# Loading x in fp32 by the hardware queue, with cast and reordering on GpSimd

## The chip, the core and the metric

The kernel runs on one core of one Trainium2 chip. The core has five engines with a queue of instructions each: TensorE (PE in the profile; its weight loads are PEld), VectorE (DVE), ScalarE (ACT), GpSimd (POOL) and SyncE (SP), which here only issues transfers. Sixteen DMA engines move data between the chip's main memory (DRAM) and the on-chip memory (SBUF, 96 or 128 partitions of a tile at a time). Matrix products land in a third memory, PSUM, from which ACT and DVE evict them. The metric is device time in microseconds (us) for one execution; less is better.

## What is computed

```python
x: 8 x 3072 x 256, fp32
X = np.fft.fft(x, axis=1)
X = np.fft.fft(X, axis=2)
h0 = X.real.astype(np.float32).reshape(24576, 256)
h = np.maximum(np.maximum(h0 @ w1, h0 @ w2), h0 @ w3)     # w1, w2, w3: 256 x 768
out = (h @ w_out).astype(np.float32)                      # w_out: 768 x 256
```

A two-dimensional Fourier transform of each of 8 batches, of which the real part is kept, is followed by a layer that takes the maximum of three products, and by an output product.

## The kernel before

**Tiling of the transform.** The 3072 rows of a batch are split as 24 x 128 (`a`, `bb`) and the 256 features as 4 x 64 (`g`, `dl`). The tile x0 holds one batch in bf16: partition g*24 + a (96 of them), and in each partition 128 rows of 64 features. A transform over `a` is a product with a 96 x 96 block matrix, `m24blk`. The function `fnet` does it with 64 matmuls (L270), one for each of the 64 features: the 128 values of that feature in x0 are the weights, which TensorE loads first (PEld L270), and `m24blk` is what streams through them, 96 columns. Before the change the weights of one matmul lie 64 elements, 128 bytes, apart. Five matmuls (in the last but one group, four) fill one PSUM tile, and ACT copies it to the tile ub (L272); there are 13 such groups in a batch and two PSUM buffers. DVE then adds and subtracts mirrored features ("folds", L280 to L297) to give zE and zO, TensorE multiplies these by cosine and sine tables (L318 to L334, again with strided weights, steps of 24 and 26 elements), and ACT evicts tE and tO (L329). POOL makes reversed copies of both, tEr and tOr (L339, L340).

**The layers.** In the main loop each batch has three blocks of 512 positions. `unit_plus`, `unit_minus` and `unit_out` compute the three-way maximum for a block and its mirror: 512-column matmuls L349, L350 and L357, an ACT eviction with Relu into stmp (L363) and a DVE maximum (L364) of a PSUM tile and stmp into hp and hm. `l2_block` makes the output product of a finished block (L367, L369, L372: 256 columns each); DVE copies the result to ot (L392, four buffers) and SP stores it (L399). These second-layer matmuls wait in a list, `l2_queue`, and are issued between the matmuls of the next block and the next batch's transform.

**Preparation.** Before the first batch DVE and ACT make the tables (`m24blk`, cos_t, sin_t, nsin_t, md) from index tiles that POOL writes (kidx, dvec). `prep_first` and `prep_second` fold the feature transform into the weights: DVE differences v_bf (L228), matmuls L232, ACT evictions, and a DVE scaling gD (L237).

**Loading x.** `load_x0` issues 16 transfers for a batch from POOL's queue (L105): four chunks of 32 rows, each for four feature groups, 96 KB each in DRAM. The runs that lie together in DRAM are 64 features of fp32, 256 bytes, and the transfer itself turns them into bf16. There are two x0 tiles, so batch b+2 is loaded when the transform of batch b has read its tile. At the start POOL's order is written out by hand (`tc.manual_schedule`): the first x chunk, the two index tiles, the other x chunks, six weight transfers (L139), w_out (L142), and batch 1's x. Elsewhere a scheduler at build time fixes the order of every engine's queue from dependencies and program order; at run time each queue is executed in that order.

Of the kernel before, what the change touches and what calls it, by code (L numbers as in the profile page):

```python
# [9 lines left out]
FP32 = mybir.dt.float32  # L10
BF16 = mybir.dt.bfloat16
# [2 lines left out]
ALU = mybir.AluOpType  # L14

ROUND = 12582912.0


def _cond_sub(nc, pool, v, thresh, tag):
# [15 lines left out]
def kernel(  # L35
# [16 lines left out]
    nc = tc.nc  # L52

    B, S, D = x.shape
# [11 lines left out]
    ps_f = ctx.enter_context(tc.tile_pool(name="ps_f", bufs=2, space=bass.MemoryType.PSUM))  # L66
    ps_l1 = ctx.enter_context(tc.tile_pool(name="ps_l1", bufs=2, space=bass.MemoryType.PSUM))
    ps_o = ctx.enter_context(tc.tile_pool(name="ps_o", bufs=2, space=bass.MemoryType.PSUM))
    x0_pool = ctx.enter_context(tc.tile_pool(name="x0", bufs=2))
    u_pool = ctx.enter_context(tc.tile_pool(name="ubuf", bufs=1))  # L70
    z_pool = ctx.enter_context(tc.tile_pool(name="zbuf", bufs=1))
    t_pool = ctx.enter_context(tc.tile_pool(name="tbuf", bufs=2))
    h_pool = ctx.enter_context(tc.tile_pool(name="hbuf", bufs=2))
    out_pool = ctx.enter_context(tc.tile_pool(name="outbuf", bufs=4))

    m24blk = consts.tile([96, 96], BF16, tag="m24blk")
    md = [consts.tile([128, 256], BF16, name=f"md{fc}", tag=f"md{fc}") for fc in range(2)]
# [16 lines left out]
    dif = consts.tile([128, 1], FP32, tag="dif")  # L94
    t_mid = consts.tile([128, 2, B], BF16, tag="t_mid")

    def load_x0(b, between):
        x0 = x0_pool.tile([96, 128 * 64], BF16, name="x0", tag="x0")
        xr = x[b].rearrange("(a bb) (g dl) -> g a bb dl", bb=128, g=4)
        x0v = x0.rearrange("p (bb dl) -> p bb dl", dl=64)  # L100
        for ch in range(4):
            if ch in between:
                between[ch]()
            for g in range(4):
                nc.gpsimd.dma_start(  # L105
                    out=x0v[g * 24:(g + 1) * 24, ch * 32:(ch + 1) * 32, :],
                    in_=xr[g, :, ch * 32:(ch + 1) * 32, :])
        return x0

    gen_pool_cm = tc.tile_pool(name="gen", bufs=1)  # L110
    gen = gen_pool_cm.__enter__()
# [11 lines left out]
    kidx = gen.tile([128, 13 * 128], FP32, tag="kidx")  # L123
    dvec = gen.tile([128, 128], FP32, tag="dvec")

    def between():

        nc.gpsimd.iota(kidx, [[1, 13], [24, 128]], base=0, channel_multiplier=0,
                       allow_small_or_imprecise_dtypes=True)
        nc.gpsimd.iota(dvec, [[1, 64], [64, 2]], base=0, channel_multiplier=0,  # L130
                       allow_small_or_imprecise_dtypes=True)

    with tc.manual_schedule(engines={mybir.EngineType.Pool}):
        x0_tiles = {0: load_x0(0, {1: between})}


        for jh in range(2):
            for wsrc, wdst in ((moe_w1, w1_bf), (moe_w2, w2_bf), (moe_w3, w3_bf)):
                nc.gpsimd.dma_start(  # L139
                    out=wdst.rearrange("p (fc j) -> p fc j", fc=2)[:, :, jh * 384:(jh + 1) * 384],  # L140
                    in_=wsrc.rearrange("(fc p) j -> p fc j", fc=2)[:, :, jh * 384:(jh + 1) * 384])
        nc.gpsimd.dma_start(out=wout_bf.rearrange("p (jc c) -> p jc c", jc=NJC),  # L142
                            in_=moe_w_out.rearrange("(jc p) c -> p jc c", jc=NJC))
        x0_tiles[1] = load_x0(1, {})


    amod = gen.tile([96, 1], FP32, tag="amod")
    nc.vector.tensor_copy(amod, pidx[0:96])
# [24 lines left out]
    for (dst, shift) in ((cos_t, 768.0), (sin_t, 0.0)):  # L173
        v = gen.tile([128, 13 * 128], FP32, name="v", tag="v", bufs=2)
        q = gen.tile([128, 13 * 128], FP32, name="q", tag="q", bufs=2)
        nc.vector.tensor_scalar(out=v, in0=kidx, scalar1=pidx, scalar2=shift,
                                op0=ALU.mult, op1=ALU.add)
        nc.vector.tensor_scalar(out=q, in0=v, scalar1=1.0 / 3072.0, scalar2=ROUND,
                                op0=ALU.mult, op1=ALU.add)
        nc.vector.tensor_scalar(out=q, in0=q, scalar1=ROUND, scalar2=-3072.0,  # L180
                                op0=ALU.subtract, op1=ALU.mult)
        nc.vector.tensor_tensor(out=v, in0=v, in1=q, op=ALU.add)
        nc.scalar.activation(out=dst, in_=v, func=AX.Sin,
                             scale=float(2.0 * math.pi / 3072.0))
    nc.vector.tensor_scalar(out=nsin_t, in0=sin_t, scalar1=-1.0, scalar2=None,
                            op0=ALU.mult)

# [22 lines left out]
                            op0=ALU.mult, op1=ALU.add)  # L210
    nc.vector.tensor_scalar(out=dif, in0=sgn, scalar1=1.0, scalar2=None, op0=ALU.subtract)
    gen_pool_cm.__exit__(None, None, None)

    zO_tiles = [consts.tile([128, 128 * 26], BF16, name=f"zO{i}", tag=f"zO{i}")
                for i in range(1)]
# [4 lines left out]
    def prep_first():  # L220

        for jh in range(2):
            cs = slice(jh * 384, (jh + 1) * 384)
            for i, (wv, vv) in enumerate(((w2_bf, v2_bf), (w3_bf, v3_bf))):
                w3d, v3d, w13d = (t.rearrange("p (fc j) -> p fc j", fc=2)[:, :, cs]
                                  for t in (wv, vv, w1_bf))
                tc.keep_in_program_order(
                    nc.vector.tensor_tensor(out=v3d, in0=w3d, in1=w13d, op=ALU.subtract))  # L228
                for (half, dst) in ((0, gE[i]), (1, gO[i])):
                    psg = ps_f.tile([128, 512], FP32, name="psg", tag="ps")  # L230
                    for fc in range(2):
                        nc.tensor.matmul(  # L232
                            psg[:, 0:384], md[fc][:, half * 128:(half + 1) * 128],
                            vv[:, fc * DFF + jh * 384: fc * DFF + jh * 384 + 384],
                            start=(fc == 0), stop=(fc == 1))
                    nc.scalar.copy(out=dst[:, cs], in_=psg[:, 0:384])
                nc.vector.tensor_scalar(out=gD[i][:, cs], in0=gO[i][:, cs], scalar1=dif,  # L237
                                        scalar2=None, op0=ALU.mult)
# [23 lines left out]
                                op0=ALU.mult)  # L262

    def fnet(b, x0):
        x0r = x0.rearrange("p (bb dl) -> p bb dl", dl=64)
        ub = u_pool.tile([128, 64 * 96], BF16, name="ub", tag="ub")
        for (d0, d1) in DLS:
            ps1 = ps_f.tile([128, 512], FP32, name="ps1", tag="ps")
            for i in range(d1 - d0):
                nc.tensor.matmul(ps1[:, i * 96:(i + 1) * 96], x0r[:, :, d0 + i], m24blk,  # L270
                                 start=True, stop=True)
            nc.scalar.copy(out=ub[:, d0 * 96:d1 * 96], in_=ps1[:, 0:(d1 - d0) * 96])  # L272

# [79 lines left out]
    def unit_minus(pses, to, jc):  # L353

        js = slice(jc * 128, (jc + 1) * 128)
        for i, pse in enumerate(pses):
            nc.tensor.matmul(pse, gD[i][:, js], to, start=False, stop=True,  # L357
                             skip_group_check=True)

    def unit_out(pses, dst, n):  # L360
        stmp = h_pool.tile([128, TOKB], BF16, name="stmp", tag="stmp")
        src3 = pses[1][:, 0:n]
        nc.scalar.activation(out=stmp[:, 0:n], in_=pses[0][:, 0:n], func=AX.Relu)  # L363
        nc.vector.tensor_tensor(out=dst, in0=src3, in1=stmp[:, 0:n], op=ALU.max)  # L364
# [53 lines left out]
    def l2_some(n):  # L418
        while n > 0 and l2_queue:
            try:  # L420
                next(l2_queue[0])
                n -= 1
            except StopIteration:
                l2_queue.pop(0)

    for b in range(B):
        tt = fnet(b, x0_tiles.pop(b))
        if b == 0:
            prep_first()
        tE, tO = tt[0]  # L430
        prev = None

        def finish(prev):
            pses, to, jc, hm = prev
            unit_minus(pses, to, jc)
            unit_out(pses, hm[:, jc, ::-1], TOKB)

        for blk in range(3):
            cs = slice(blk * TOKB, (blk + 1) * TOKB)
            hp = h_pool.tile([128, NJC, TOKB], BF16, name="hp", tag="hp")  # L440
            hm = h_pool.tile([128, NJC, TOKB], BF16, name="hm", tag="hm")
            for jc in range(NJC):
                pses = unit_plus(tE[:, cs], tO[:, cs], jc, TOKB)
                unit_out(pses, hp[:, jc, :], TOKB)
                if prev is not None:
                    finish(prev)
                prev = (pses, tO[:, cs], jc, hm)
                l2_some(11)
            l2_some(1000)
            if blk == 2:  # L450
                finish(prev)
            if b == 0 and blk == 0:
                prep_second()
            l2_queue.append(l2_block(b, blk, hp, hm, tt))
            if blk == 0 and b + 2 < B:
                x0_tiles[b + 2] = load_x0(b + 2, {})
            if blk == 1 and b == B - 1:
                l2_queue.append(l2_mid())

# [30 lines left out]
```

## Time and profile before

| What | Value |
|---|---|
| median of 3 runs | 500.57 us (499.67 to 501.51) |
| span of the profiled execution, first to last instruction | 497.1 us |
| mean granted TensorE clock | 0.993 |
| x transfers on POOL, L105 | 128, 109.5 us busy |
| first matmul of the transform, L270 | starts at 27.46 us |
| x0 matmuls, L270 | 512, 57.4 us busy |
| POOL copies tEr, L339 | 8, 1471 ns each |
| folds, L280, zE and zO | 160, 260 to 473 ns each |
| store issues on SP, L399 | 208, median 431 ns |

A row of the profile has a source line, the engine, the operation, the tile it writes and the tile it reads, their shapes, and how often it occurs; then the busy time in us, the mean duration of one in ns, and the engine's idle time just before with what ended it. Matmuls are pipelined, so one's duration is longer than its distance to the next; the distance of their starts is what TensorE pays. The page also shows the span in 40 slices of 12.4 us, with a digit for the busy tenths of each. A timeline row begins with the start and the duration in us, and ends, in brackets, with idle time and its releaser. 3.5 us of the runs' median lie outside the profiled span.

### The profile page before, as it was taken

The page shows a single profiled execution, that of the slowest core. Times are in us where ns is not written, and L with a number is a line of the kernel's source. Part 1 is how long each engine was busy: PE and PEld are TensorE (multiplying, and loading weights), DVE is VectorE, ACT ScalarE, POOL GpSimd, SP SyncE. Part 2 cuts the span into 40 slices and gives each one's busy share as a digit, 9 for nine tenths or more (in the row PEclk, how much of TensorE's full clock was granted, in tenths as well). Part 3 has the DMA queues.
Part 4 walks back from the last instruction along what each step waited for, and adds up shares of the span by engine and source line. Part 5 has one row for each costly group of instructions (what it writes and reads, how often), then busy time and mean ns, then how long its engine had stood idle before and what let it go on. Part 6 is the DMA issues. An engine that isn't in the chain of part 4 may idle for free.

```text
span 497.1 us, 9195 instructions
## 1 busy us (share of the span) xinstructions
PE 453.5 (91%) x3408; PEld 315.6 (63%) x3408; DVE 320.4 (64%) x662; ACT 260.9 (52%) x472; POOL 140.6 (28%) x160
## 2 busy tenths in 40 slices
PE   0056999999999999999999999999999999999995
PEld 0055447785568657785669666875669566866664
DVE  8834674657676576657666567657675666667663
ACT  1355652575436653575446644665457644765440
POOL 9979800029000750029000840048000100020000
PEclk9999899999999999999999999999999999999998
DMA  8999992219921692219911793119911022102122
GB/s 48 75 164 99 98 32 86 84 44 108 105 86 66 59 133 99 73 44 109 126 65 65 74 123 102 65 46 120 134 64 65 22 65 84 65 22 65 65 84 86
DMA packets 163436, 40.05 MB, mean 81 GB/s; under 512 B 136512, under 2 KB 163392, under 8 KB 163392
## 3 DMA queue, kind: packets, MB, share of 16 engines
q0 software_dynamic: 135536, 14.30, 70.6%
q1 hardware_dynamic: 27856, 25.18, 16.1%
q8 instruction: 26, 0.43, 0.4%
q14 instruction: 18, 0.15, 0.1%
HBM read 28.31 MB, written 25.17 MB: 108 GB/s over the span
## 4 chain that ended last, share of the span: by engine, by line
PE 78%; DVE 3%; ACT 2%; POOL 2%; DMA 1%; issue 1%; DVEq 0%; ACTq 0%
PE po L372 23%; PE pse L349 12%; PE pse L357 11%; PE pse L350 11%; PE ps L270 8%; PE po L367 4%; PE po L369 4%; POOL x L105 2%; PE ps L318 2%; DMA x<-in_x_dram 1%; PE ps L324 1%; PE ps L326 1%; ACT stmp L363 1%; PE ps L321 1%; DVE zE L280 1%
## 5 line engine op out<-in xcount | busy, mean ns | idle before, releaser
L363 ACT ACTIVATE stmp<-pse 128x512 bf16<-128x512 f32 (+1 forms) x294 | 167.7, 588 | 164.3 <-PE pse L350 128.6
L364 DVE TENSOR_TENSOR hp<-pse,stmp 128x512 bf16<-128x512 f32 x144 | 99.1, 690 | 99.1 <-PE pse L357 39.8
L105 POOL DMA_DIRECT2D x<-in_x_dram x128 | 109.5, 863 | 8.1 <-DMA x<-in_x_dram 3.6
L349 PE MATMUL pse<-tE,gE 128*128 128x512 bf16 x288 | 108.8, 379 | 1.7 <-DVE hm L364 0.7
L350 PE MATMUL pse<-tO,gO 128*128 128x512 bf16 x288 | 109.1, 380 | 0.0
L364 DVE TENSOR_TENSOR hm<-pse,stmp 128x512 bf16<-128x512 f32 x144 | 99.0, 687 | 11.8 <-ACT stmp L363 9.3
L357 PE MATMUL pse<-tO,gD 128*128 128x512 bf16 x288 | 94.8, 380 | 1.1 <-ACT stmp L363 0.6
L339 POOL COPY tEr<-tE 128x1536 bf16<-128x1536 bf16 x8 | 11.8, 1471 | 289.1 <-ACT tE L329 289.1
L372 PE MATMUL po<-wout_bf,hp 128*128 128x256 bf16 x576 | 92.6, 272 | 0.0
L372 PE MATMUL po<-wout_bf,hm 128*128 128x256 bf16 x576 | 89.1, 272 | 0.1
L270 PE MATMUL ps<-m24blk,x 96*128 96x96 bf16 x512 | 57.4, 250 | 28.8 <-DMA w_bf<-in_moe_w_dram 27.5
L270 PEld LDWEIGHTS <-x 96*128 96x128 bf16 x512 | 55.9, 199 | 33.1 <-DMA w_bf<-in_moe_w_dram 27.4
L392 DVE COPY ot<-po 128x512 f32<-128x512 f32 x96 | 65.5, 684 | 14.5 <-PE po L372 13.8
L372 PEld LDWEIGHTS <-hm 128*128 128x128 bf16 x576 | 56.1, 99 | 17.3 <-DVE hm L364 0.4
L372 PEld LDWEIGHTS <-hp 128*128 128x128 bf16 x576 | 56.2, 100 | 14.2
L272 ACT CAST ub<-ps 128x480 bf16<-128x480 f32 (+1 forms) x104 | 55.4, 554 | 15.6 <-PE ps L270 13.3
L357 PEld LDWEIGHTS <-gD 128*128 128x128 bf16 x288 | 28.1, 98 | 29.8 <-issue 1.5
L350 PEld LDWEIGHTS <-gO 128*128 128x128 bf16 x300 | 29.4, 98 | 27.1 <-issue 12.2
L349 PEld LDWEIGHTS <-gE 128*128 128x128 bf16 x300 | 29.5, 99 | 21.1 <-issue 2.6
L280 DVE TENSOR_TENSOR zE<-ub 128x240 bf16<-128x240 bf16 (+2 forms) x80 | 20.2, 311 | 33.9 <-ACT ub L272 33.9
L367 PE MATMUL po<-gw,tE 128*128 128x256 bf16 x96 | 26.2, 272 | 0.0
L369 PE MATMUL po<-gwr,tOr 128*128 128x256 bf16 x96 | 26.2, 272 | 0.0
(99 smaller groups left out, 359.5 us busy)
## 6 DMA issues: line engine op xcount, KB each, us to landing
out_dram<-ot SPq DMA_DIRECT2D x176, 128.0 KB, 1.7
x<-in_x_dram POOLq DMA_DIRECT2D x128, 96.0 KB, 6.7
out_dram<-ot SPq DMA_DIRECT2D x24, 64.0 KB, 6.7
w_bf<-in_moe_w_dram POOLq DMA_DIRECT2D x6, 192.0 KB, 6.2
out_dram<-ot SPq DMA_DIRECT2D x8, 63.0 KB
wout_bf<-in_moe_w_out_dram POOLq DMA_DIRECT2D x1, 384.0 KB, 8.6
out_dram<-ot SPq DMA_DIRECT2D x1, 8.0 KB
```

Source lines behind the costliest of these rows:

```text
L105: nc.gpsimd.dma_start(out=x0v[g * 24:(g + 1) * 24, ch * 32:(ch + 1) * 32, :], in_=xr[g, :, ch * 32:(ch + 1) * 32, :])
L270: nc.tensor.matmul(ps1[:, i * 96:(i + 1) * 96], x0r[:, :, d0 + i], m24blk, start=True, stop=True)
L272: nc.scalar.copy(out=ub[:, d0 * 96:d1 * 96], in_=ps1[:, 0:(d1 - d0) * 96])
L349: nc.tensor.matmul(pse[:, 0:n], gE[i][:, js], te, start=True, stop=False)
L350: nc.tensor.matmul(pse[:, 0:n], gO[i][:, js], to, start=False, stop=True)
L357: nc.tensor.matmul(pse, gD[i][:, js], to, start=False, stop=True, skip_group_check=True)
L363: nc.scalar.activation(out=stmp[:, 0:n], in_=pses[0][:, 0:n], func=AX.Relu)
L364: nc.vector.tensor_tensor(out=dst, in0=src3, in1=stmp[:, 0:n], op=ALU.max)
L367: nc.tensor.matmul(po, te, gw[:, 0:256], start=True, stop=False)
L369: nc.tensor.matmul(po, to, wo, start=False, stop=False)
L372: nc.tensor.matmul(po, hcols(jc), wout_bf[:, jc * 256:(jc + 1) * 256], start=False, stop=(jc == NJC - 1))
L392: nc.vector.tensor_copy(out=ot, in_=po)
```

## The change

x is loaded in fp32 by SP's queue into a new tile xs, one for each chunk (four buffers, 96 x 2048). `cast_x` copies a chunk into x0 as bf16 and writes it with features outermost and the 128 rows adjacent, so that the 128 weights of one L270 matmul lie side by side. POOL does the casts, except for 44 of the 64 features of chunk 3 of batch 0, which DVE does. At the start the index tiles come first on POOL; the weight transfers stay on POOL and follow the casts. Batch 1's load waits for the last weight transfer. In the loop, batch b+1 is cast and batch b+2 loaded after block 0 of batch b. The pools of hp, hm, stmp and ot are opened after the preparation's temporary tiles have been given back.

```diff
+AFTER = mybir.DependencyInfo(mybir.DependencyClass.Sync, mybir.DependencyReason.DATA)
...
+    xs_pool = ctx.enter_context(tc.tile_pool(name="xs", bufs=4))
...
-    h_pool = ctx.enter_context(tc.tile_pool(name="hbuf", bufs=2))
-    out_pool = ctx.enter_context(tc.tile_pool(name="outbuf", bufs=4))
...
-    def load_x0(b, between):
-        x0 = x0_pool.tile([96, 128 * 64], BF16, name="x0", tag="x0")
+    def load_x(b, after=None):
+        chunks = []
         xr = x[b].rearrange("(a bb) (g dl) -> g a bb dl", bb=128, g=4)
-        x0v = x0.rearrange("p (bb dl) -> p bb dl", dl=64)
         for ch in range(4):
-            if ch in between:
-                between[ch]()
+            xs = xs_pool.tile([96, 32 * 64], FP32, name="xs", tag="xs")
+            xsv = xs.rearrange("p (bb dl) -> p bb dl", dl=64)
             for g in range(4):
-                nc.gpsimd.dma_start(
-                    out=x0v[g * 24:(g + 1) * 24, ch * 32:(ch + 1) * 32, :],
+                ld = nc.sync.dma_start(
+                    out=xsv[g * 24:(g + 1) * 24],
                     in_=xr[g, :, ch * 32:(ch + 1) * 32, :])
-        return x0
+                if after is not None:
+                    tc.add_manual_dep(ld.ins, after.ins.name, AFTER, reason="weights first")
+            chunks.append(xs)
+        return chunks
+
+    def cast_x(x0, ch, xs, engine, d0=0, d1=64):
+
+        dst = x0.rearrange("p (dl bb) -> p dl bb", bb=128)[:, d0:d1, ch * 32:(ch + 1) * 32]
+        src = xs.rearrange("p (bb dl) -> p dl bb", dl=64)[:, d0:d1, :]
+        if engine is nc.scalar:
+            engine.copy(out=dst, in_=src)
+        else:
+            engine.tensor_copy(dst, src)
+
+    def new_x0():
+        return x0_pool.tile([96, 64 * 128], BF16, name="x0", tag="x0")
...
+    raw = {0: load_x(0)}
+    x0_tiles = {0: new_x0()}
+
+    with tc.manual_schedule(engines={mybir.EngineType.Pool}):
         nc.gpsimd.iota(kidx, [[1, 13], [24, 128]], base=0, channel_multiplier=0,
                        allow_small_or_imprecise_dtypes=True)
         nc.gpsimd.iota(dvec, [[1, 64], [64, 2]], base=0, channel_multiplier=0,
                        allow_small_or_imprecise_dtypes=True)
-
-    with tc.manual_schedule(engines={mybir.EngineType.Pool}):
-        x0_tiles = {0: load_x0(0, {1: between})}
+        for ch in range(3):
+            cast_x(x0_tiles[0], ch, raw[0][ch], nc.gpsimd)
         for jh in range(2):
             for wsrc, wdst in ((moe_w1, w1_bf), (moe_w2, w2_bf), (moe_w3, w3_bf)):
-                nc.gpsimd.dma_start(
+                wld = nc.gpsimd.dma_start(
...
+            if jh == 0:
+                cast_x(x0_tiles[0], 3, raw[0][3], nc.gpsimd, 44, 64)
         nc.gpsimd.dma_start(out=wout_bf.rearrange("p (jc c) -> p jc c", jc=NJC),
                             in_=moe_w_out.rearrange("(jc p) c -> p jc c", jc=NJC))
-        x0_tiles[1] = load_x0(1, {})
...
+    cast_x(x0_tiles[0], 3, raw.pop(0)[3], nc.vector, 0, 44)
+    raw[1] = load_x(1, after=wld)
+
     nc.vector.tensor_scalar(out=nsin_t, in0=sin_t, scalar1=-1.0, scalar2=None,
                             op0=ALU.mult)
...
     gen_pool_cm.__exit__(None, None, None)
+    h_pool = ctx.enter_context(tc.tile_pool(name="hbuf", bufs=2))
+    out_pool = ctx.enter_context(tc.tile_pool(name="outbuf", bufs=4))
...
     def fnet(b, x0):
-        x0r = x0.rearrange("p (bb dl) -> p bb dl", dl=64)
+        x0r = x0.rearrange("p (dl bb) -> p dl bb", bb=128)
...
-                nc.tensor.matmul(ps1[:, i * 96:(i + 1) * 96], x0r[:, :, d0 + i], m24blk,
+                nc.tensor.matmul(ps1[:, i * 96:(i + 1) * 96], x0r[:, d0 + i, :], m24blk,
                                  start=True, stop=True)
...
-            if blk == 0 and b + 2 < B:
-                x0_tiles[b + 2] = load_x0(b + 2, {})
+            if blk == 0 and b + 1 < B:
+                x0_tiles[b + 1] = new_x0()
+                for ch, xs in enumerate(raw.pop(b + 1)):
+                    cast_x(x0_tiles[b + 1], ch, xs, nc.gpsimd)
+                if b + 2 < B:
+                    raw[b + 2] = load_x(b + 2)
```

More of the change, by code (lines that the diff above doesn't have):

```diff
@@ L124 @@
     dvec = gen.tile([128, 128], FP32, tag="dvec")
-    def between():
+    raw = {0: load_x(0)}
+    x0_tiles = {0: new_x0()}
+    with tc.manual_schedule(engines={mybir.EngineType.Pool}):
         nc.gpsimd.iota(kidx, [[1, 13], [24, 128]], base=0, channel_multiplier=0,
```

## The prediction

> **What bounds the kernel now.** I read four views, from the whole to the single instruction. First the page: busy time by engine and the span in 40 slices.
>
> ```profile
> PE 453.5 (91%) x3408; PEld 315.6 (63%) x3408; DVE 320.4 (64%) x662; ACT 260.9 (52%) x472; POOL 140.6 (28%) x160
> ...
> PE   0056999999999999999999999999999999999995
> ...
> POOL 9979800029000750029000840048000100020000
> ```
>
> The reader should see two regimes. TensorE (PE) does nothing for two slices (12.4 us each), half work for two, and is then full to the end. So a microsecond is saved either before about 53 us, or by making TensorE's own work shorter; POOL is idle two thirds of the time and bounds nothing after the start. The chain of waits says the same: 78% of it is PE.
>
> Second, the timeline of the first 48 us, POOL, PE and DVE:
>
> ```profile
> 7.24 15.68 POOL L105 DMA_DIRECT2D x<-in_x_dram  x12
> ...
> 22.91 4.27 POOL L139 DMA_DIRECT2D w_bf<-in_moe_w_dram  x6
> 27.23 0.83 POOL L142 DMA_DIRECT2D wout_bf<-in_moe_w_out_dram  x1
> 27.43 1.04 PEld L270 LDWEIGHTS <-x 96*128 96x128 bf16 x11 [27.43 <-DMA w_bf<-in_moe_w_dram]
> ...
> 44.73 3.21 DVE L237 TENSOR_SCALAR gD<-gO,dif 128x384 bf16<-128x384 bf16 x1 [6.00 <-ACT gO L236]
> 44.94 1.48 POOL L339 COPY tEr<-tE 128x1536 bf16<-128x1536 bf16 x1
> 46.35 1.47 POOL L340 COPY tOr<-tO 128x1536 bf16<-128x1536 bf16 x1
> ```
>
> PE starts at 27.4 us. The page names a weight DMA as releaser, but L270 does not read weights: it needs the last of sixteen x transfers, whose issue on POOL ends at 22.9 us and which lands some 4.5 us later (median for x: 6.7 us). Issue by POOL sets the start. The gD row matters later: the other three gD took 0.31 to 0.47 us, this one 3.21, and it ended when POOL's two copies did.
>
> Third, the steady state, where the first Fourier step (L270) of batch 3 runs between second-layer matmuls (L372):
>
> ```profile
> 210.00 0.57 PE L270 MATMUL ps<-m24blk,x 96*128 96x96 bf16 x5
> 210.41 0.27 PE L369 MATMUL po<-gwr,tOr 128*128 128x256 bf16 x1
> 210.52 0.38 PE L372 MATMUL po<-wout_bf,hm 128*128 128x256 bf16 x2
> 210.74 0.57 PE L270 MATMUL ps<-m24blk,x 96*128 96x96 bf16 x5
> 211.14 0.28 PE L372 MATMUL po<-wout_bf,hm 128*128 128x256 bf16 x1
> 211.26 0.57 PE L270 MATMUL ps<-m24blk,x 96*128 96x96 bf16 x5
> ...
> 210.08 1.08 ACT L272 CAST ub<-ps 128x480 bf16<-128x480 f32 x2 [0.17 <-PE ps L270]
> ```
>
> Two groups of five take 210.00 to 211.26 = 1.26 us and hold four matmuls of 256 columns at 0.109 us (0.436). The ten small ones take the other 0.82, so 0.082 each, twice what their columns need (96/256 x 0.109 = 0.041). ACT evicts the pair in 1.08 and waits 0.17 for PE. PE is the bound here, and in it the weight load. Fourth, the page's groups of weight loads:
>
> ```profile
> L270 PEld LDWEIGHTS <-x 96*128 96x128 bf16 x512 | 55.9, 199 | 33.1 <-DMA w_bf<-in_moe_w_dram 27.4
> ...
> L372 PEld LDWEIGHTS <-hm 128*128 128x128 bf16 x576 | 56.1, 99 | 17.3 <-DVE hm L364 0.4
> ```
>
> The x weights are read with a step of 64 elements (128 bytes) and take 199 ns; hm's, adjacent, take 99.
>
> **The change, part by part.**
>
> Removed: 128 x issues of 0.81 to 0.86 us on POOL (109.5 us). In the steady state they are off the path. The spacing of the tEr copies gives the batch period: 54.7 and 54.8 us in the last two batches with loads, 54.4 in the one without. I take 0.35 us for five periods, **-1.8 us** (bounds 0, and -4.9 from the mean of all five loaded periods, 55.4).
>
> Row and feature order swapped: L270 now reads 128 adjacent weights. No row shows this at 96 partitions. Weights with a 52-byte step (zO) follow one another every 0.066 us even when 64 columns or one are multiplied; adjacent weights should be no slower. With 0.066 a pair takes 0.66 + 0.436 = 1.10 us, just above ACT's 1.08. That is -0.16 per pair, 6.5 pairs a batch: -1.04, and for seven batches **-7.3 us** (bounds: 0 if the step is not the cause; with ACT as the bound 0.18 x 6.5 x 7 = -8.2). In batch 0 a pair takes 1.25 us with PE and ACT waiting for each other; I take 0.1 x 6.5, **-0.7** (0 to -1.0).
>
> Added on SP: 128 issues. The nearest row, a store issue, is 0.43 us; sixteen are 6.9 us and not the limit. How fast small rows land is: a batch is 96 x 128 = 12,288 runs of 256 bytes. Lower bound: POOL issued 13 transfers of a batch at 0.81 us without waiting, 16 x 0.81 = 12.9 us. Upper: 70.6% x 16 x 497.1 us / 135,536 packets = 41.4 ns a packet, on 16 engines 31.8 us. In between, the last three issues of a batch (122.18, 123.36, 124.48) came 1.15 us apart, two of them after waiting for an x DMA: 18.4 us a batch, which I take, being the same runs. From 1.0 us, with 1.7 us to land (a store's), chunks arrive at 7.3, 11.9, 16.5 and 21.1 us.
>
> Added on POOL: casts of 96 x 2048. The tEr copy gives 1470 ns / 1536 elements, so 1.96 us at least; the source has a step of 256 bytes, and the only stepped-to-adjacent ratio in the trace is the weight load's, 209 ns (median for x) to 99, 2.1, so 4.1 us at most. The step is what sets this copy apart, so I take 4.1. [...]
>
> Start: iotas end by 3.9 us (no x issue ahead of them). Casts run 7.3-11.4, 11.9-16.0, 16.5-20.6; three weight issues of 0.71 to 22.7; POOL's 20/64 of chunk 3, 1.3 us, to 24.0. VectorE (DVE) casts 44/64 of it, 1408 elements: at the row of the 128x256 conversions (0.29 us) 1.6 us, doubled for the step 3.3, so 21.1 to 24.4. Ahead of it stands DVE's table chain, 9.4 us (9.23 to 18.65 now), which can begin near 6 us. If it slips between casts it costs nothing; if every cast locks it out it ends at 6 + 9.4 + 12.3 = 27.7 and PE starts at 31. I take 24.4 plus one table operation of 1.1: 25.5, **-1.9 us** (bounds: load 12.9 us gives 18.9, -8.5; load 31.8 gives 37.8, +10.4). The rest of the weights leave POOL by 27 us and land by 33; L228 reads them at 38 now, so they stay hidden with 3 us to spare. The load of batch 1, behind them on SP, takes to about 52; its use is at 96.
>
> Next in line is preparation: v_bf and gD, eight DVE operations between 38 and 56 us that PE waits for. Batch 1's casts can fall there. I put in half a cast, **+2.0** (0 to 8.2, two casts).
>
> Steady: four casts, 16.4 us, are free if they follow tOr (111.4 to 127.8 in batch 1), as the x issues do now: between 106 and 155 us DVE reads PSUM as one input and makes no folds. SP now waits for each cast before it loads the next chunk, with stores behind it; three output copies (105.9, 114.8, 120.7) fall in that time, and there are four buffers. Zero for both.
>
> Sum: -1.8 - 7.3 - 0.7 - 1.9 + 2.0 = -9.7; span 497.1 to 487.4. The median of the runs is 3.5 us over the profiled span: **490.9 us**. Own range of this case 484 to 497.
>
> **Rivals.**
>
> *The load is quick* (18.9 us to PE): 490.9 - 6.6 = 484. For: the issues of 0.81 us on POOL are gone, and a store on SP issues in 0.43. Against: the waits on x DMA at the end of each issue burst.
>
> *The weight step is not the cause*: 490.9 + 8.0 = 499. For: 199 ns is latency, and loads overlap. Against: the 0.082 us pitch.
>
> *Casts hold the folds* (the slower side). DVE's folds (L280) end PE's wait for L318, and the cover is spent: PE idles 0.41 us there already (104.6 to 105.04). If the casts of a later batch stand ahead of tEr on POOL, they meet the folds at 104, and gD shows DVE held through two POOL copies in a row. One cast a batch: 4.1 x 6 = +24.6, 516 us; all four: +98. It decides from 2.0 us a batch on. Against: the x issues now stand behind tOr although their buffer is free at 103. [...]
>
> *The load is slow* (31.8 us): PE starts at 37.8, 490.9 + 12.3 = 503.
>
> *SP holds the stores*: one cast beyond the four buffers, again 4.1 x 6, 515.
>
> That a later x arrives too late for its cast is excluded by 55 us of lead.
>
> **How the numbers follow.** Forecast 0.48, quick load 0.12, step not the cause 0.10, folds held 0.15, slow load 0.11, stores held 0.04. Predicted is the forecast's 491. Leaving out the two cases near 515 leaves 0.81: 481 to 508, with the spread of the others. A difference under 0.5% (2.5 us) can't be told from none: faster 0.62 (forecast, quick load, a little of the third), same 0.13, slower 0.25.
>
> **What would show it.** PE's first L270 at 25.5 us; L270 pairs of 1.10 us and PEld of x near 99 ns; POOL casts of 4.1 us, after tOr; folds still 0.26 to 0.47 us; period near 53. It is wrong if a fold row has a maximum of microseconds, if PE waits for ot, or if the x loads on SP land more than 2 us apart.

## The result and the profile after

| | median of the runs | ratio to the kernel before (95%) | span of the profiled run, clock |
|---|---|---|---|
| before | 500.87 us (4 runs) | | 497.1 us, 0.993 |
| after | 526.86 us (519.5 to 530.6, 4 runs) | 1.0424 [1.0362, 1.0485] | 528.8 us, 0.940 |

The changed kernel is slower by 4.2%, where 491 us was predicted. The ratio goes by the two runs at 519.5 and 523.4 us (mean 521.4, clock 0.955 and 0.949); the profile is of a slower run, at 530.6 us, so the 31.7 us that its span is longer than the 497.1 before show where time goes, and what each cause is worth is taken from the experiments.

The page of the changed kernel, engines and 40 slices (13.2 us each):

```profile
span 528.8 us, 9309 instructions
...
PE 453.2 (86%) x3408; PEld 310.1 (59%) x3408; DVE 339.3 (64%) x663; ACT 260.6 (49%) x472; POOL 150.6 (28%) x64
...
PE   0045499979998899979997999989997999999995
...
PEclk9999679969999799979998899979997999999999
```

PE's busy time is the same as before (453.5), but not its place. The row of nines now has a hole early (the 4 in slice 5) and a dip that comes back every 4.4 slices, which is a batch period; below each, the granted clock falls too.

Three marks place the loss: the first matmul of the second Fourier step (L318 before, L336 after), the starts of the tEr copies, and the end. To the first mark +3.3 us (37.30 to 40.59); on to the second tEr +7.4; from there five periods of 58.1 against 55.4, +13.6; the sixth +6.8; the end +0.6. Together 31.7. One more count is needed: up to the second tEr PE now ran 96 second-layer matmuls and not 167, and in the sixth period 264 and not 191. These 71 to 73, at 0.109 us each, are 7.8 us put off from one to the other. So preparation with batch 1's transform lost about 15 us, the steady periods 13.6, the start 3.3, and the sixth period by itself won about 1.

**The start.** The timeline of POOL and DVE up to the first x matmul (start, duration, engine, line):

```profile
9.10 10.14 POOL L119 CAST x<-xs 96x2048 bf16<-96x2048 f32 x2 [5.57 <-DMA xs<-in_x_dram]
20.75 4.13 POOL L119 CAST x<-xs 96x2048 bf16<-96x2048 f32 x1 [1.50 <-DMA xs<-in_x_dram]
...
12.11 7.45 DVE L182 TENSOR_SCALAR m24blk<-t,ind_g 96x24 bf16<-96x24 f32 x4
...
21.28 3.68 DVE L211 TENSOR_SCALAR vm<-dvec,pf 128x128 f32<-128x128 f32 x1
...
26.45 2.12 DVE L221 CAST vm<-vi 128x256 f32<-128x256 int32 x1
...
29.55 1.43 DVE L119 CAST x<-xs 96x1408 bf16<-96x1408 f32 x1
...
31.13 0.96 PE L288 MATMUL ps<-m24blk,x 96*128 96x96 bf16 x10 [31.13 <-DVE x L119]
```

Small table operations end when POOL's casts end (19.24, 24.88, and 28.41 for its 20/64 of chunk 3): two of the four m24blk operations take 3.6 us each, the other two 0.22. DVE's own part of chunk 3 stands behind them, at 29.55, and PE starts at 31.13 in place of 27.46. The load is late as well: the last packet of chunk 3 lands at 25.3, where the prediction had 21.1.

**Preparation.** DVE, and then PE, in the same kernel:

```profile
47.97 3.75 DVE L255 TENSOR_SCALAR gD<-gO,dif 128x384 bf16<-128x384 bf16 x1 [5.96 <-ACT gO L254]
51.64 3.97 DVE L246 TENSOR_TENSOR v_bf<-w_bf 128x768 bf16<-128x768 bf16 x1
57.65 3.33 DVE L255 TENSOR_SCALAR gD<-gO,dif 128x384 bf16<-128x384 bf16 x1 [2.04 <-ACT gO L254]
...
55.66 1.44 PE L250 MATMUL psg<-v_bf,md 128*128 128x384 bf16 x4 [7.01 <-DVE v_bf L246]
...
67.11 1.44 PE L250 MATMUL psg<-v_bf,md 128*128 128x384 bf16 x4 [2.67 <-DVE v_bf L246]
```

Four of the eight operations take 3.3 to 4.0 us, as long as a cast: three of the four gD (the other takes 0.31) and one of the four v_bf (the others take 0.54). PE stops for 7.01, 2.03 and 2.67 us.

**Steady state.** The end of batch 4's transform on PE, and the windows of the same period (columns: busy time and instruction count of PE, PEld, DVE, ACT, POOL; then granted clock, DMA share, GB/s):

```profile
284.45 0.84 PE L288 MATMUL ps<-m24blk,x 96*128 96x96 bf16 x10 [0.58 <-ACT ub L290]
285.47 0.84 PE L288 MATMUL ps<-m24blk,x 96*128 96x96 bf16 x10 [0.18 <-ACT ub L290]
...
289.54 0.33 PE L336 MATMUL ps<-cos_t,zE 128*128 128x128 bf16 x1 [1.66 <-DVE zE L310]
```

```profile
278.43:283.26 4.83, 4.46 (x40) 2.52 (x39) 3.33 (x6) 4.56 (x9) 0.00 (x0) 1.00 0.89 234
283.26:288.10 4.84, 3.17 (x40) 2.13 (x39) 4.38 (x14) 4.76 (x11) 0.00 (x0) 0.97 0.11 36
288.10:292.94 4.84, 3.40 (x30) 3.12 (x31) 3.19 (x17) 2.13 (x4) 0.00 (x0) 0.50 0.16 54
```

Before, four second-layer matmuls stood in each pair of x groups. Here none does. PE waits for ACT after every ten, 1.02 us a pair (ACT's pace), then 1.66 for the last fold. With the four in it a pair takes 1.02 us too (e1 below, 164.87 to 165.89), so there they fill time in which PE would wait. Here they run elsewhere, and the wait stays; in the last window the clock is 0.50, and zE's matmuls follow one another every 0.107 us where 0.066 to 0.07 is usual. The order of PE, written at build time, has no second-layer matmul among the x matmuls of batches 1 to 6, and 24 again in batch 7, before which no x load stands on SP.

**What went as predicted.** The weight loads and the casts, from the page:

```profile
L119 POOL CAST x<-xs 96x2048 bf16<-96x2048 f32 (+1 forms) x32 | 118.8, 3740 | 72.0 <-DMA xs<-in_x_dram 36.6
...
L288 PEld LDWEIGHTS <-x 96*128 96x128 bf16 x512 | 31.9, 103 | 58.7 <-issue 52.4
```

199 ns have become 103, as hm's 99.

### The profile page after: what moved, and what is told of

The parts are those of the page before. It is cut to its first block, busy times and chain, and to the rows that moved or that the text cites. A ratio compares the mean times of both kernels' runs of the same rounds, so it can differ in the third digit from the quotient of the medians.

```text
span 528.8 us, 9309 instructions
## 1 busy us (share of the span) xinstructions
PE 453.2 (86%) x3408; PEld 310.1 (59%) x3408; DVE 339.3 (64%) x663; ACT 260.6 (49%) x472; POOL 150.6 (28%) x64
## 4 chain that ended last, share of the span: by engine, by line
PE 78%; DVE 9%; ACT 9%; issue 2%; POOL 0%; DVEq 0%; POOLq 0%; ACTq 0%
PE po L390 24%; PE pse L367 12%; PE pse L368 11%; PE pse L375 11%; ACT ub L290 7%; PE po L385 4%; PE po L387 4%; PE ps L288 2%; PE ps L336 2%; ACT stmp L381 2%; PE ps L342 2%; PE ps L344 2%; PE ps L339 2%; DVE m24blk L182 1%; DVE zE L298 1%
## 5 line engine op out<-in xcount | busy, mean ns | idle before, releaser
L381 ACT ACTIVATE stmp<-pse 128x512 bf16<-128x512 f32 (+1 forms) x294 | 170.9, 590 | 179.2 <-PE pse L368 143.9
L382 DVE TENSOR_TENSOR hp<-pse,stmp 128x512 bf16<-128x512 f32 x144 | 98.8, 690 | 103.3 <-PE pse L375 82.0
L119 POOL CAST x<-xs 96x2048 bf16<-96x2048 f32 (+1 forms) x32 | 118.8, 3740 | 72.0 <-DMA xs<-in_x_dram 36.6
L367 PE MATMUL pse<-tE,gE 128*128 128x512 bf16 x288 | 112.9, 393 | 1.2 <-ACT stmp L381 0.3
L382 DVE TENSOR_TENSOR hm<-pse,stmp 128x512 bf16<-128x512 f32 x144 | 99.2, 689 | 5.1 <-PE pse L375 2.4
L375 PE MATMUL pse<-tO,gD 128*128 128x512 bf16 x288 | 92.0, 383 | 2.6 <-DVE hp L382 2.4
L390 PE MATMUL po<-wout_bf,hp 128*128 128x256 bf16 x576 | 86.2, 273 | 0.0
L390 PE MATMUL po<-wout_bf,hm 128*128 128x256 bf16 x576 | 86.1, 273 | 0.0
L288 PE MATMUL ps<-m24blk,x 96*128 96x96 bf16 x512 | 40.8, 216 | 41.4 <-DVE x L119 31.1
L288 PEld LDWEIGHTS <-x 96*128 96x128 bf16 x512 | 31.9, 103 | 58.7 <-issue 52.4
L290 ACT CAST ub<-ps 128x480 bf16<-128x480 f32 (+1 forms) x104 | 54.1, 560 | 4.8 <-PE ps L288 3.4
L336 PE MATMUL ps<-cos_t,zE 128*128 128x128 bf16 (+1 forms) x104 | 20.9, 293 | 11.8 <-DVE zE L310 11.6
L385 PE MATMUL po<-gw,tEr 128*128 128x256 bf16 x96 | 26.2, 273 | 0.0
```

What stands on the lines that cost most here:

```text
L119: engine.tensor_copy(dst, src)
L288: nc.tensor.matmul(ps1[:, i * 96:(i + 1) * 96], x0r[:, d0 + i, :], m24blk, start=True, stop=True)
L336: nc.tensor.matmul(outsl, er[:, :, r], cos_t[:, k0:k0 + w], start=True, stop=not two)
L367: nc.tensor.matmul(pse[:, 0:n], gE[i][:, js], te, start=True, stop=False)
L385: nc.tensor.matmul(po, te, gw[:, 0:256], start=True, stop=False)
L390: nc.tensor.matmul(po, hcols(jc), wout_bf[:, jc * 256:(jc + 1) * 256], start=False, stop=(jc == NJC - 1))
```

## The experiments

All ratios are against runs of the kernel before, beside each. "Period" is from one tEr copy to the next.

**e1_late_load**: batch b+2's load stands after block 2, not block 0; casts stay.

```diff
-                if b + 2 < B:
-                    raw[b + 2] = load_x(b + 2)
+            if blk == 2 and b + 2 < B:
+                raw[b + 2] = load_x(b + 2)
```

> The changed kernel with one thing moved: batch b+2's x loads stand in the program after block 2 of batch b instead of after block 0. Theory (order): the loads held the stores on SP, and so second-layer matmuls were left out of the transform when the order was fixed; here 24 of them stand between the L288 groups again. Batch period 58.1 -> 53.5 to 54, no clock below 0.98 after 80 us, total about 496 to 499; what is left over 500.9 minus the weight gain is the start. Rival (contention at run time of casts and x transfers with the other work): the period stays at 57 to 58 and the total within 3 us of the changed kernel's 521.

512.44 us, 1.0263 [1.023, 1.0295]. The order has its 24 matmuls back in every x stage, and the period is 55.4 in place of 58.1. From the first to the second tEr it is still 76.2 (before: 62.9). The steady loss is tied to where the loads stand on SP; the early one is not. The period of 53.5 to 54 and the total of 496 to 499 that were expected are both missed: something else keeps the steady period at 55.4 (e13), and the early loss was counted too low.

**e2_out8**: `out_pool` with eight buffers in place of four, in the changed kernel.

> The changed kernel with eight output buffers (ot) instead of four, loads where they are. Theory (order, and through the buffers that wait for their stores): second-layer matmuls return to the transform from batch 2 on (24 in it and 8 after it), batch 1 stays without them; period 54 from batch 2, total about 500 to 503. Rival (stores late at run time, or contention): with the same transfers and casts the period stays at 57 to 58, total near 521.

521.01 us, 1.0427 [1.0405, 1.045]; period 57.0. These are the rival's figures, though its reason is not shown by them. From batch 2 the x stage has 24 matmuls, as the theory said, but 44 matmuls of the first layer now run in a row without any, and only 8 second-layer matmuls, not 14, stand before the second Fourier step. PE idles 2.6 us a batch, against 1.3 in e1: 0.8 of it for the last fold, most of the rest among the first layer. More buffers move the hole.

**e3_before_adjacent**: the kernel before, reading x0 as if rows were adjacent (x0 itself is still written row by row, so x values are mixed up).

```diff
-        x0r = x0.rearrange("p (bb dl) -> p bb dl", dl=64)
+        x0r = x0.rearrange("p (dl bb) -> p dl bb", bb=128)
...
-                nc.tensor.matmul(ps1[:, i * 96:(i + 1) * 96], x0r[:, :, d0 + i], m24blk,
+                nc.tensor.matmul(ps1[:, i * 96:(i + 1) * 96], x0r[:, d0 + i, :], m24blk,
```

> The kernel before, whose first transform step reads each weight set from 128 adjacent elements of x0 as it was loaded (features and rows of x are thereby mixed up; same number of instructions and bytes, no cast, no SP load). If the step of the weights costs TensorE time: L270 pitch 0.042 instead of 0.082, pair 1.26 -> 1.02 to 1.10, total 500.9 -> 488 to 492. If not: 500 to 501.

482.92 us, 0.9663 [0.9649, 0.9677]; period 53.4 to 54.1 against 54.4 to 56.4. PEld falls to 101 ns. Of the 15.9 us of span that it wins, 7.4 lie before the second tEr and are partly the experiment's own, since its first groups need fewer chunks and PE starts at 19.8; the steady part is about 1.5 us a batch.

**e4_late_noswap**: e1 with a cast that keeps row order.

```diff
-        dst = x0.rearrange("p (dl bb) -> p dl bb", bb=128)[:, d0:d1, ch * 32:(ch + 1) * 32]
-        src = xs.rearrange("p (bb dl) -> p dl bb", dl=64)[:, d0:d1, :]
+        dst = x0.rearrange("p (bb dl) -> p bb dl", dl=64)[:, ch * 32:(ch + 1) * 32, d0:d1]
+        src = xs.rearrange("p (bb dl) -> p bb dl", dl=64)[:, :, d0:d1]
```

> e1 without the swap: cast in the order of the source, weights 128 bytes apart again. If adjacent weights are worth what the pair says (0.16 to 0.24 us x 6.5 x 7): 7 to 11 us above e1, about 505 to 509. POOL's cast, now adjacent to adjacent, tells what the step costs it: 1.96 us by the copy's rate, against 3.7 in the changed kernel. If the step of the weights is not the cause: equal to e1 within 2 us.

509.85 us, 1.0208 [1.0181, 1.0234]: steady period 57.0 (1.6 longer), but first to second tEr 65.8 (10.4 shorter), with casts of 1.89 us. The total is 2.6 us under e1, where 7 to 11 above it was expected, because the shorter cast holds less of the preparation; the swap pays later.

**e5_start**: e1, batch 0 loaded as before the change, with the cast in POOL's transfer and no swap for it.

```diff
-    raw = {0: load_x(0)}
-    x0_tiles = {0: new_x0()}
+    raw = {}
...
+        x0_tiles = {0: load_x0(0, {1: between})}
-        for ch in range(3):
-            cast_x(x0_tiles[0], ch, raw[0][ch], nc.gpsimd)
...
-    cast_x(x0_tiles[0], 3, raw.pop(0)[3], nc.vector, 0, 44)
```

> The late-load kernel (512.4 us), with batch 0 alone loaded as before the change: by POOL's queue with the cast in the transfer, row order kept, no cast on POOL or DVE ahead of the first x matmul. Theory A (the casts hold DVE's table operations, so the start): first x matmul back at 27.5 us (30.5 in the late-load kernel), 509.5 us. Rival B (the start is lost to the load and tables are free): no change in the table operations' times, start above 30 us. Rival C (what is won at the start is lost in preparation, since PE waits there for v_bf and gD, which the casts of batch 1 hold and which do not move): 512 us, with the first tEr earlier but the second tEr at the same 119 to 120 us.

508.04 us, 1.0175 [1.0141, 1.021]. The first x matmul is at 27.73, and the four m24blk operations take 0.66 us together (4.06 in e1, 7.45 in the changed kernel). 4.4 us won, somewhat over A's 3: first to second tEr also shrinks, from 76.2 to 74.1. The edit takes away the slower load and the casts together, so it does not tell A from B. The traces of e1 and then e4 say more (DVE's part of chunk 3):

```profile
27.52 2.85 DVE L119 CAST x<-xs 96x1408 bf16<-96x1408 f32 x1
```

```profile
27.69 0.89 DVE L119 CAST x<-xs 96x1408 bf16<-96x1408 f32 x1 [7.05 <-DMA xs<-in_x_dram]
```

In e4, with casts half as long, DVE has its tables done and idles 7.05 us for the load, and PE starts at 28.72. So 1.3 of the changed kernel's 3.7 us are there without a held table, and the other 2.4 come with the longer casts: by held tables in the changed kernel (29.55), by DVE's own long cast in e1.

**e6_prep**: e1, batch 1's casts wait for the last preparation operation of DVE.

```diff
-                prep_second()
+                ready = prep_second()
...
-                    cast_x(x0_tiles[b + 1], ch, xs, nc.gpsimd)
+                    cp = cast_x(x0_tiles[b + 1], ch, xs, nc.gpsimd)
+                    if b == 0:
+                        tc.add_manual_dep(cp.ins, ready.ins.name, AFTER, reason="prep first")
```

> The late-load kernel, with the four casts of batch 1 made to wait until the preparation of the second layer (v_bf, gD, gw, gwr on DVE) is done; nothing else changed. Theory A (the 13 us between first and second tEr are DVE's two-input operations held by POOL's casts): v_bf back to 0.6 us, gD to 0.5 us, the period from the first to the second tEr falls from 76.2 to about 62, total 498 to 500 us, steady period unchanged at 55.4. Rival B (PE is slow there because its order has no second-layer work to fill in, whatever DVE does): the period stays at 72 or more, total above 508. Rival C (casts come too late for batch 1's x matmuls now): v_bf short, but PE then waits for the casts at the start of batch 1, period near 70.

500.03 us, 1.0007 [0.9991, 1.0023]. Its timeline, DVE and POOL:

```profile
47.79 0.32 DVE L255 TENSOR_SCALAR gD<-gO,dif 128x384 bf16<-128x384 bf16 x1 [5.78 <-ACT gO L254]
48.02 0.56 DVE L246 TENSOR_TENSOR v_bf<-w_bf 128x768 bf16<-128x768 bf16 x1
...
63.13 14.74 POOL L119 CAST x<-xs 96x2048 bf16<-96x2048 f32 x4 [15.28 <-DVE gwr L279]
108.33 1.47 POOL L357 COPY tEr<-tE 128x1536 bf16<-128x1536 bf16 x1 [30.46 <-ACT tE L347]
```

Only the casts moved, by 16 us, and all gD take 0.31 to 0.32. In e1 they took 2.5 to 3.8, while its v_bf were already at 0.55: there the held operation was gD, and v_bf waited behind it. First to second tEr is 64.4 (62 was expected), with the same 168 second-layer matmuls as in e1, 11.8 us less. The preparation's loss is shown.

**e7_both**: the edits of e5 and e6 together.

> Both edits at once: batch 0 loaded as before, and batch 1's casts after the preparation. If start and preparation are separate losses they add: 3 us and 13 us off 512.4, 496.4 us, under the kernel before (499.7) by the 0.66%. If one hides in the other: 498 to 500. If neither is the cause: 509 and more.

496.60 us, 0.9935 [0.9913, 0.9956]: the losses add (4.4 and 12.4 off 512.4 make 495.6), and the kernel is faster than before by 0.65%.

**e8_x_on_pool**: the changed kernel with its x loads on POOL's queue.

```diff
-                ld = nc.sync.dma_start(
+                ld = nc.gpsimd.dma_start(
```

> The changed kernel with one word altered: the x loads are issued on POOL's queue in place of SP's; fp32 landing, casts, waits and their places are the same. The PE order written at build time has its 24 second-layer matmuls in every first Fourier step again. Theory A (the 3 us a batch are lost through the order, which the loads on SP between the stores spoil): steady period 55.4 us in place of 58.05, as with the late load. Rival B (the 3 us are the casts' own, through DVE or the clock): steady period 58. The start is later in both, since POOL issues sixteen loads ahead of the first cast (some 33 us to the first x matmul) and batch 1's load is issued on it as well.

591.26 us, 1.1828 [1.1789, 1.1867], periods 65.7 to 67.9 in batches with a load behind them. Neither theory. DVE on the timeline in one period (11.6 us of such waits from 190 to 255 us):

```profile
249.12 0.69 DVE L410 COPY ot<-po 128x512 f32<-128x512 f32 x1 [9.95 <-DMA out_dram<-ot]
```

The order was the good one, but POOL issued sixteen loads right behind the casts (222 to 241 us), and no output buffer came free until 249: a wait for stores that the changed kernel does not have. So this run could not price the order.

**e9_bare_x**: e6 with PE's order alone altered.

```diff
+        l2_some(1000)
         tt = fnet(b, x0_tiles.pop(b))
...
+                if last_po[0] is not None and d0 + i == 0:
+                    tc.add_manual_dep(mm.ins, last_po[0].ins.name, ORDER, reason="order")
```

> The late-load kernel with batch 1's casts after the preparation (500.0 us, steady period 55.4), with one thing altered, the order of PE: the 24 + 38 second-layer matmuls that it runs within and behind the first Fourier step of a batch are all issued ahead of it, so that the 64 x matmuls of a batch stand alone, as the changed kernel has them in batches 1 to 6. Loads, casts and stores stay where they are. Theory A (the order alone makes the 3 us a batch that the changed kernel loses): PE waits for ACT's evictions and for the last fold, the granted clock falls at the end of the period, period 58 to 59, total 518 to 526. Rival B (the 3 us come from x loads and stores meeting on SP, and the order follows from it without a price): period 55.4 to 56, total under 505.

547.67 us, 1.0958 [1.0931, 1.0985]. Windows at the end of a period:

```profile
354.00:358.00 4.00, 2.91 (x41) 2.12 (x40) 1.91 (x6) 4.00 (x9) 0.00 (x0) 1.00 1.01 139
358.00:361.00 3.00, 1.17 (x13) 0.73 (x9) 2.41 (x14) 1.73 (x4) 0.00 (x0) 0.53 0.99 125
361.00:364.43 3.43, 3.21 (x30) 3.15 (x31) 0.94 (x8) 1.76 (x3) 0.00 (x0) 0.50 0.89 136
```

The same picture as in the changed kernel: ACT full while the x matmuls run, then PE mostly idle for the last fold, then the clock at 0.5. The period is 62.1, 6.7 over e6's, where 58 to 59 was expected: the mechanism is shown, its price was taken too low. The changed kernel pays less for its bare stage, perhaps since some of its x matmuls run earlier, among the units (eight and seven at a time from 281.46), and since e9 runs 64 second-layer matmuls in one row ahead of them; that was not tried.

**e10_both_out8**: e7 with eight output buffers.

> The kernel with both edits (batch 0 loaded as before, batch 1's casts after the preparation; 496.6 us) with eight output buffers in place of four. The order of PE written at build time then has 20 units of the second and third block without second-layer matmuls between them, in place of 30, and the same 24 + 14 around the first Fourier step. Theory A (the idle 1.3 us a batch is the bare units'): 0.4 us a batch back, 493.5 to 495 us, period 55.0. Rival B (the idle time is DVE's or ACT's own): no change, 496 to 497.

508.76 us, 1.0186 [1.0163, 1.021]; periods 57 to 58.6 from the third on. Missed, and on the other side. PE's row:

```profile
317.25 0.39 PE L396 MATMUL po<-gw,tE 128*128 128x256 bf16 x1 [1.64 <-DVE ot L421]
```

Behind the 20 bare units 32 second-layer matmuls follow in a row, PE waits for DVE to empty their PSUM tile, and the clock is 0.69 in that window. An order with fewer bare units is not a better one if what is held back comes in a lump.

**e11_both_noswap**: e7 with e4's cast.

> The kernel with both edits (496.6 us), but the cast keeps row and feature order, so that the x weights are read with a step of 128 bytes again in all batches and POOL's cast reads and writes adjacent elements. What the swap itself is worth once nothing collides. Theory A (0.16 us for each pair of groups, 1.6 us a batch, as the late-load kernel gave against its unswapped form): period 57.0, total 507 to 508. Rival B (half of those 1.6 us were the casts' own length): period 56.2 or less, total under 503.

507.01 us, 1.0148 [1.0123, 1.0174]; period 56.95 against 55.39: theory A, on both numbers. The page of e11:

```profile
L132 POOL CAST x<-xs 96x2048 bf16<-96x2048 f32 x28 | 52.3, 1890 | 40.7 <-DMA xs<-in_x_dram 25.4
...
L298 PEld LDWEIGHTS <-x 96*128 96x128 bf16 x512 | 54.9, 200 | 30.8 <-DMA w_bf<-in_moe_w_dram 27.6
```

The swap is worth 10.4 us, 1.56 a batch, although its cast is twice as long (3.72 to 3.74 us in e7).

**e12_even_order**: e7 with stores on POOL's queue, eight output buffers, and the last block's second-layer matmuls ordered between the next batch's x groups.

```diff
+        if after is not None:
+            tc.add_manual_dep(mm.ins, after.ins.name, ORDER, reason="order")
...
-                nc.sync.dma_start(out=out[row: row + 24 * (p1 - p0 - 1) + 1: 24, :],
+                nc.gpsimd.dma_start(out=out[row: row + 24 * (p1 - p0 - 1) + 1: 24, :],
```

> The kernel with both edits (496.6 us), made to have an even order of PE: the output is stored through POOL's queue, so that the x loads have SP to themselves, with eight output buffers, and the second-layer matmuls of a batch's last block are ordered behind the next batch's x groups. Every six units then have 9 or 11 second-layer matmuls behind them and the x stage has 18 + 15. Theory A (what is left over the kernel with adjacent weights alone is order): period 53.5 to 54.2, total 484 to 489. Rival B (stores on POOL stand behind casts of 3.7 us, and output buffers run out, or DVE is held more often): period above 55.5, total above 498.

562.08 us, 1.1239 [1.1209, 1.127]. PE over two periods (245 to 370 us):

```profile
L304 PE MATMUL ps<-m24blk,x 96*128 96x96 bf16 x128 | 12.7, 257 | 17.9 <-POOL x L134 17.8
```

POOL's order put two of the four casts behind the stores of the third block, and PE waited 8.9 us a batch for them. B's side, by a wait that neither theory named.

**e13_even_order_casts_first**: e12 with POOL's order in the main loop written by hand, and the loads back at block 0, where the change has them.

```diff
+    with tc.manual_schedule(engines={mybir.EngineType.Pool}):
         for b in range(B):
...
-            if blk == 2 and b + 2 < B:
+            if blk == 0 and b + 2 < B:
```

> The run before with POOL's order written by hand: the four casts of the next batch stand together, right behind the four output copies that follow tOr, and the loads of the batch after are issued behind them on SP, which has nothing else. The order of PE is the same even one. Theory A (the 1.9 us a batch left over are the order of PE): PE does not wait for a cast, period 53.5 to 54.5, total 484 to 491. Rival B (they are a price of the casts, by DVE or by stores that wait behind them): period 55.4 or more, total 496 or more, with PE's idle time put down to DVE (ot, hp or hm) while the casts run.

486.57 us, 0.9736 [0.9703, 0.9769], period 53.7. PE in the x stage:

```profile
307.81 0.37 PE L304 MATMUL ps<-m24blk,x 96*128 96x96 bf16 x5
308.02 0.38 PE L409 MATMUL po<-wout_bf,hp 128*128 128x256 bf16 x2
308.28 0.37 PE L304 MATMUL ps<-m24blk,x 96*128 96x96 bf16 x5
```

From batch 1 on casts and loads are those of the change; the order is even, and the period is that of e3 (53.4 to 54.1), which has no casts (and an order of its own). No cost of the casts shows in the steady state. That the 1.7 us under e7's 55.4 are order fits the trace: PE idles 1.1 us a period ahead of first-layer matmuls in e7, where 30 units stand without second-layer matmuls, and 0.0 in e13 (which has 0.6 ahead of its x matmuls, e7 0.1). But stores and buffers changed with the order, so its share was not measured by itself. This version is 2.6% faster than the kernel before.

## Why the prediction was wrong

- **The step that failed: "Steady: four casts, 16.4 us, are free if they follow tOr"**, and "Zero for both". The casts were free: after batch 0 PE waits for none. What it left out is that a load on SP changes the order of PE, since the order of all queues is fixed at build time. I looked at SP for stores that would be late; DVE never waited for an output buffer. Price in the profile: 13.6 us; e1 gets 9.0 of the 521.4 us back. e1 and e8 restore the order by taking the loads away from between the stores; e9 has the loss without touching loads or casts. That the scheduler holds the second layer back because it counts on late stores fits e2, where more buffers bring the 24 matmuls back, but was not tried by itself.
- **The second: "I put in half a cast" for preparation, +2.0 (0 to 8.2).** It cost about 15 us in the profile, outside its bounds. gD's row was read rightly, but the chain alternates: PE and ACT must answer between DVE's operations, so a next operation met the next cast, over all four. Nor was PE's slower clock after a stop of 7 us priced (0.55 to 0.74 from 56 to 74 us). e6 gave 12.4 us back.
- **The start, -1.9, came out at +3.7.** Chunks land 5.9 us apart (4.6 taken), and the casts hold table operations (two of the four m24blk 3.6 us each, the others 0.22), the first cast itself taking 6.59 us, the second 3.63. PE's 31.13 equals the 31 that was named for a start with the tables held by every cast, but partly by luck: that case had the load on time. Load and casts were not divided in the changed kernel; e4's trace puts 1.3 us on the load. e5 gave 4.4 us back.
- **Right in mechanism, too small: the weights.** 1.04 us a batch were predicted; e7 against e11 has 1.56. With adjacent weights the pitch is 0.042, what the columns need, not the 0.066 of zO's stepped weights, so ACT sets the pair, and at 1.02 us, not 1.08: 1.26 - 1.02 = 0.24, and 6.5 of these are the 1.56.
- **The 1.8 us for POOL's removed issues** do not show: in e3, which keeps them, the one period without x issues is the longest (54.1 against 53.4 to 54.0).
- **The cast's 4.1 us** measured 3.73 undisturbed.
- **Rivals.** Folds were not held (longest 471 ns; they are done before the casts begin), stores were not held, and the load was slower than forecast (23.6 us from batch 0's first packet to its last, 18.4 taken) but not the 31.8 of its rival; a transfer reads 192 KB in DRAM, and the 96 KB given for it above are what landed as bf16. The slower side of the forecast was DVE held by casts in the folds; DVE was held, but in preparation: the one v_bf that met a cast took 3.97 us, 0.55 without. What a cast does to a fold the changed kernel does not show, since they never met.

## What to carry to other kernels

Moving a transfer to another queue can change the order of engines that never touch it, when a scheduler writes the order at build time: before counting waits, compare the order of the engine that bounds the kernel, and look whether the short stage still has its filler. Here a cast on POOL cost nothing beside DVE's maxima from PSUM (0.69 us with and without it), and in preparation held an operation of DVE on SBUF that it met for about its own length (3.3 to 4.0 us in all, 0.31 to 0.56 without); price every stage it can fall into, preparation too, and hold it back by one dependency if it meets a chain of such operations. With that, the late load and the old start the kernel is at 496.6 us; the 486.6 came with stores on POOL, eight output buffers and an order written by hand.

## What was not expected of the hardware

- A swapped cast of 96 x 2048 takes POOL 3.73 us, one in order 1.89.
- Besides v_bf, operations of DVE with one input tile and a column of scalars were held: gD took 3.75 us for 0.32, as its row before the change had hinted, and four m24blk operations of 96 x 24 7.45 for 0.66. Maxima that read PSUM and one SBUF tile (L382) ran at 0.69 us beside casts as without them.
- While sixteen loads with 256-byte runs, issued on POOL's queue in one burst (e8, 222 to 241 us), were under way, the output buffer that DVE had filled by 233.3 us, four copies earlier, came free at 249.1, when its stores on SP's queue had landed: 15.8 us, where the median store of that run lands 1.8 us after its issue. What held them was not tried.
